# Splitting the second row tile's statistics, issuing the first weights behind a warming product, and a shorter warming, in a one-core spectral filter and gated MLP kernel

## The chip, the cores and the metric

The kernel runs on one core of one Trainium2 chip. The metric is device time in microseconds (us) of one launch. The kernel before takes 171.04 us, the median of three runs from 170.93 to 171.09.

## What is computed

The input is 2048 rows of 512 values in bfloat16. Every row is normalised, and two branches work on the normalised rows: a two-dimensional Fourier filter and a gated feed-forward block with 1792 hidden columns. The result is their sum with the input.

```python
def reference(A_x, A_w_r, A_w_i, B_x, B_w_gate, B_w_up, B_w_down):
    def _A_ref(x, w_r, w_i):
        X = rfft2(x.astype(float32)) * (w_r + 1j * w_i)
        return irfft2(X, s=(S, D)).astype(bfloat16)

    def _B_ref(x, w_gate, w_up, w_down):
        g = einsum("bsd,df->bsf", x, w_gate)
        u = einsum("bsd,df->bsf", x, w_up)
        return einsum("bsf,fd->bsd", gelu(g) * u, w_down)

    x = A_x
    xn = (x - mean(x)) / sqrt(var(x) + 1e-5)
    return x + _A_ref(xn, A_w_r, A_w_i) + _B_ref(xn, B_w_gate, B_w_up, B_w_down)
```

## The kernel before

The 2048 rows are 16 row tiles of 128 rows; four row tiles make a block. A row tile passes through these steps: a load (`rows`, issued at L461), its mean and variance (`stats`: bn_stats at L511, bn_aggr at L512), the reciprocal root of the variance, the normalising (L528), and a transposition, which puts the 512 columns on the partitions as `xnT`. From `xnT` TensorE makes the gate and up products (L722 for the first three hidden chunks of the first two row tiles, L703 for all others), ScalarE takes them out of PSUM (GELU of the gate at L736 and L708, a copy of the up product at L737 and L709), VectorE multiplies them (L738, L710), and the down products follow (L751). The Fourier branch is short matrix products (L612, L835, L839, L916, L917, L976) with ScalarE evictions and long VectorE butterflies (all recorded at the helper line L465).

No order is written out by hand. Each step is one `op` with an engine, a planned cost, a key and what it reads and writes; `_Sched.run` gives every engine a fixed order from these, and `emit` puts in the semaphore waits. For a load, `land` is a planned landing time: it shapes the order and is no wait. A change of a cost, a key or a dependency can so reorder instructions far from its place.

The start is what the change touches:

- `warm` (L474): products of a constant with itself, ten of 512 columns and one of 256, which nobody reads. They run on TensorE before its first input has arrived.
- Queue of ScalarE: the identity for the transpositions, then the first weights, `wg` and `wu` with 384 columns each (`wload`, 384 KB each), then the Sqrt table, with no wait between the three loads.
- Queue of SP: row tiles 0 and 1 at once; row tiles 2 and 3 behind the fourth warming product (`gate`), then the following weight columns 384 to 768, 768 to 1024 and 1024 to 1280.
- Row tile 0: `root_act` takes the root on ScalarE (L516) and the reciprocal on VectorE (L518). `first_half` normalises half of the columns (L561), transposes them on TensorE (L558) and copies them to `xnT`, the first half on VectorE (L566), the second on ScalarE (L564).
- Row tile 1: `stats`, `root_act`, `norm` (L528), `turn` (transposes at L541, copy at L546), and then its products at L722.
- The GELU table is loaded on ScalarE at L626.

The order of VectorE at the start is: bn_stats and bn_aggr of tile 0, bn_stats of tile 1, reciprocal of tile 0, bn_aggr of tile 1, two half normalisings of tile 0, reciprocal of tile 1, copy of tile 0's first half, normalising of tile 1, copy of tile 1. The order of TensorE is: warming, four transposes of tile 0, two gate products, four transposes of tile 1, the other 22 products of tile 0 (gate chunks 0 to 2, then up chunks 0 to 2), 24 products of tile 1, then L703.

Of the kernel before, what the change touches and what calls it, by code (L numbers as in the profile page):

```python
# [10 lines left out]
F32 = mybir.dt.float32  # L11
# [5 lines left out]
NFC = 14  # L17
NHALF = 10
NFIRST = 3
WARM = 10 * (512,) + (256,)  # L20
HKEY = 1.5
NORM = 20.0, 1.5
STAT = 18.0, 1.5
# [121 lines left out]
class _Sched:  # L145
# [11 lines left out]
    def op(self, eng, cost, fn, reads=(), writes=(), tiles=(), key=0.0, after=(), dma=0, lag=0.0, due=None, land=None):  # L157
        o = _Op()
        o.eng, o.fn, o.cost, o.key, o.dma, o.lag, o.due, o.land = eng, fn, cost, key, dma, lag, due, land
        o.reads, o.writes, o.tiles = reads, writes, [(t, False) for t in tiles]  # L160
        o.extra = [a for a in after if a is not None]
        o.seq = len(self.ops)
        o.end = None
        o.pos = None
        self.ops.append(o)
        return o
# [182 lines left out]
def bass_parallel_sum__spectral_gfnet__glu_gated_geglu__prompt_kernel(  # L349
# [21 lines left out]
    sch = _Sched()  # L371
    op = sch.op

    with ExitStack() as es:
        def sb(name, shape, dt=BF16, cell=0):
            n = int(np.prod(shape))
            t = es.enter_context(nc.sbuf_tensor(name, [P, n], dt))
            return view(t, name, 0, shape, cell)

        def view(t, name, lo, shape, cell=0):  # L380
            n = int(np.prod(shape))
            ap = t[:, lo:lo + n]
            if len(shape) > 1:
                names = "abcdef"[:len(shape)]
                ap = ap.rearrange("p (%s) -> p %s" % (" ".join(names), " ".join(names)), **dict(zip(names[1:], shape[1:])))
            return _V(ap, name, np.arange(lo, lo + n).reshape(shape), cell or (64 if n > 512 else 1))
# [7 lines left out]
        wg = sb("wg", [4, FF])  # L394
# [9 lines left out]
        t2 = sb("edge2", [2, 4, 2])  # L404
        eps = sb("eps", [1], F32)
        bst = sb("bst", [16, 6], F32)
        bag = sb("bag", [16, 2], F32)
        vv = sb("vpe", [16], F32)
        rs = sb("rstd", [16], F32)
# [63 lines left out]
        def warm(n):  # L473
            return op("pe", 0.000834 * n, lambda e: e.matmul(ps_dn[:, 0:n], ones[:, 0:P], ones[:, 0:n], start=True, stop=True), tiles=(wt,), key=-50)  # L474

        warms = [warm(n) for n in WARM]


        def load(q, dst, src, nbytes, **kw):
            return dma(q, dst, lambda: src, nbytes, wr=(dst,), **kw)  # L480

        def wload(q, dst, src, lo, hi, **kw):
            return load(q, dst[:, :, lo:hi], src[:, :, lo:hi], (hi - lo) * 1024, **kw)

        k = iter(np.arange(0.0, 1.0, 0.001))
        def rows(lo, hi, land=None):
            return load("sp", x[:, lo:hi], xb[:, lo:hi, :], (hi - lo) * 131072, key=next(k), land=land)

        load("act", ident, c_small.ap()[:, 0:P], 32768, key=-9)
        for w, v in ((wg, wgv), (wu, wuv)):  # L490
            wload("act", w, v, 0, 384, key=0.5, land=5.5 if w is wg else 6.4)
        rows(0, 1, 3.1)
        rows(1, 2, 3.6)
        gate.append(warms[3])
        rows(2, 3, 6.9)
        rows(3, 4, 7.2)
# [7 lines left out]
        def xs(s):  # L504
            return x[:, s]

        def xn(s):
            return RB(8192 + 512 * (s % 8), [4, P])

        def stats(s, key, due=None, after=()):  # L510
            op("dve", 0.61, lambda e: e.bn_stats(bst[:, s].ap, xs(s).ap), reads=(xs(s),), writes=(bst[:, s],), key=key, due=due, after=after)  # L511
            op("dve", 0.11, lambda e: e.bn_aggr(bag[:, s].ap, bst[:, s].ap), reads=(bst[:, s],), writes=(bag[:, s],), key=key, due=due)  # L512

        def root_act(s0, n, key):
            sl = slice(s0, s0 + n)
            op("act", 0.29, lambda e: e.activation(rs.ap[:, sl], bag.ap[:, sl, 1], ACT.Sqrt, bias=eps.ap, scale=1.0),  # L516
               reads=(bag[:, sl], eps), writes=(rs[:, sl],), key=key)
            op("dve", 0.09, lambda e: e.reciprocal(rs.ap[:, sl], rs.ap[:, sl]), reads=(rs[:, sl],), writes=(rs[:, sl],), key=key)  # L518
# [29 lines left out]
        def first_half(h):  # L548
            cs = slice(2 * h, 2 * h + 2)
            i, r, o = xs(0)[:, 256 * h:256 * h + 256], xn(0)[:, cs].rs([256]), xnT[:, 0, 0, cs].rs([256])  # L550
            t = _T("sp")

            def bank():
                return ps_sp_bf[:, t.slot * 2048:t.slot * 2048 + 256]

            def f(e):
                for j in range(2):
                    ins = e.transpose(bank()[:, j * P:(j + 1) * P], xn(0).ap[:, 2 * h + j], ident.ap)  # L558
                return ins

            op("dve", 0.2, lambda e: e.tensor_scalar(r.ap, i.ap, bag.ap[:, 0, 0:1], rs.ap[:, 0:1], SUB, MUL), reads=(i, bag[:, 0], rs[:, 0:1]), writes=(r,), key=-70.0)  # L561
            op("pe", 2 * 0.107, f, reads=(r, ident), tiles=(t,), key=-70.0, lag=0.1)
            if h:
                op("act", 0.27, lambda e: e.activation(o.ap, bank(), ACT.Copy), writes=(o,), tiles=(t,), key=-70.0)  # L564
            else:
                op("dve", 0.2, lambda e: e.tensor_copy(o.ap, bank()), writes=(o,), tiles=(t,), key=-70.0)  # L566

        def turn_dma(s):
            i, o = xn(s), xnT[:, s // 4, s % 4]
            op("sp", 1.25, lambda e: e.dma_start_transpose(o.ap, i.rs([512]).ap), reads=(i,), writes=(o,), dma=425000, key=-5.0, lag=-0.4 if s < 4 else 0.0)  # L570
# [16 lines left out]
        def fold(b):  # L587
# [15 lines left out]
            for p in {0: (), 1: (4, 6), 2: (8, 10), 3: (12, 14, 0, 2)}[b]:  # L603
                t = _T("sp")

                def f_c(e, p=p, t=t):
# [11 lines left out]
                   writes=(yv,), tiles=(t,), key=-0.5)  # L618

        stats(0, -60.0)  # L620
        stats(1, -66.0, None, (sch.ops[-1],))
        root_act(0, 1, -75.0)
        root_act(1, 1, -64.0)
        for h in range(2):
            first_half(h)
        op("act", 1.5, lambda e: e.activation(tmp.ap, eps.ap, ACT.Gelu_apprx_tanh), reads=(eps, xnT[:, 0, 0], rs[:, 0:2]), writes=(tmp,), key=-30.0)  # L626
        norm(1, -60.0)
        turn(1, 1, -60.0)
        for s in (2, 3):
            stats(s, -58.0, None, (sch.ops[-1],))  # L630
# [217 lines left out]
        for ri, f in ((0, ADD), (1, SUB)):  # L848
            op("pool", 0.3, lambda e, ri=ri, f=f: e.tensor_tensor(edge.ap[:, ri], ev[0].ap[:, ri], ev[1].ap[:, ri], f),
               reads=(ev[0][:, ri], ev[1][:, ri]), writes=(edge[:, ri],), key=1.0)  # L850
# [53 lines left out]
        for i, v in enumerate((0, 4, 1, 7, 2, 6, 3, 5)):  # L904
            t = _T("sp")

            def f_i(e, v=v, t=t):
# [15 lines left out]
               writes=(gv,), tiles=(t,), key=-0.5)  # L923
# [104 lines left out]
```

## Time and profile before

One execution was profiled. It took 171.27 us; its span, from the first to the last instruction, is 169.4 us, and the 1.9 us left lie around the span.

| what | profiled execution |
|---|---|
| time | 171.27 us |
| span | 169.4 us |
| TensorE (PE) busy | 165.2 us, 98% |
| VectorE (DVE) busy | 145.7 us, 86% |
| ScalarE (ACT) busy | 107.7 us, 64% |
| GpSimd (POOL) busy | 10.9 us, 6% |
| DMA, mean over the span | 95 GB/s |

PEld is TensorE's loading of weights, which overlaps its products. In a timeline a line has the start in us, the time in us, the engine, the source line, the operation, and what it writes and reads; idle time ahead of it and what ended that stands in square brackets. "SPq" and "ACTq" are the queues in which an engine issues transfers.

### The profile page before, as it was taken

Reading aid. Unit: us, or ns where it says so; the run is one execution under the profiler, and the core shown is the slowest. Engines: PE = TensorE matmul, PEld = TensorE weight load, DVE = VectorE, ACT = ScalarE, POOL = GpSimd, SP = SyncE. Lnnn points to the kernel's source line nnn. Section 1 sums busy time; section 2 is a strip of 40 time slices with the busy share of each in tenths; the row PEclk is TensorE's granted clock in tenths of the full one; section 3 lists DMA queues with packets and bytes.
Section 4 is the critical chain, followed back from the end, with each engine's and each line's share of the span. In section 5 each row is a group of like instructions: output and inputs, shape, how many; then the busy total and the mean of one; then the engine's idle time right before and its main releaser. Section 6 shows DMA issues by size and latency. Waiting matters only on the chain.

```text
span 169.4 us, 2755 instructions
## 1 busy us (share of the span) xinstructions
PE 165.2 (98%) x1019; PEld 88.2 (52%) x1019; DVE 145.7 (86%) x294; ACT 107.7 (64%) x182; POOL 10.9 (6%) x25
## 2 busy tenths in 40 slices
PE   8799999999999999999999999999999999999994
PEld 3488884444554654444444446455444566544443
DVE  2775999998785299999999999999999995999932
ACT  3588886663957966669494639669556399761000
POOL 2040232420000000002000000000000000000000
PEclk9999999999999999999999999999999999999999
DMA  4999999796734436350000000000000000033311
GB/s 142 340 290 198 299 291 100 227 296 128 193 74 95 93 69 134 90 196 12 2 0 0 0 4 0 0 0 4 2 0 0 0 0 4 2 127 119 130 62 62
DMA packets 24927, 16.02 MB, mean 95 GB/s; under 512 B 10957, under 2 KB 24274, under 8 KB 24914
## 3 DMA queue, kind: packets, MB, share of 16 engines
q1 hardware_dynamic: 23714, 15.03, 37.8%
q10 hardware_dynamic: 1200, 0.82, 1.6%
q8 instruction: 8, 0.13, 0.3%
q14 instruction: 5, 0.04, 0.1%
HBM read 11.38 MB, written 2.10 MB: 80 GB/s over the span
## 4 chain that ended last, share of the span: by engine, by line
PE 95%; DMA 2%; DVE 1%; SPq 0%; issue 0%; DVEq 0%
PE ps_gu L703 56%; PE ps_dn L751 21%; PE ps_sp L751 7%; PE ps_sp L612 2%; PE ps_sp L976 2%; DMA x_sb<-in_A_x_dram 2%; PE ps_sp L835 2%; PE ps_gu L722 1%; PE ps_sp L916 1%; PE ps_sp L917 1%; PE ps_dn L722 1%; DVE bst L511 0%; PE ps_sp L839 0%; PE ps_sp L541 0%; SPq L461 0%
## 5 line engine op out<-in xcount | busy, mean ns | idle before, releaser
L703 PE MATMUL ps_gu<-xnT,wu 128*128 128x512 bf16 (+1 forms) x252 | 57.3, 351 | 0.0
L703 PE MATMUL ps_gu<-xnT,wg 128*128 128x512 bf16 (+1 forms) x252 | 57.3, 350 | 0.0
L709 ACT ACTIVATE uu<-ps_gu 128x512 bf16<-128x512 f32 (+1 forms) x63 | 34.5, 548 | 12.5 <-PE ps_gu L703 11.5
L708 ACT ACTIVATE gg<-ps_gu 128x512 bf16<-128x512 f32 (+1 forms) x63 | 34.6, 550 | 11.1 <-PE ps_gu L703 9.6
L751 PE MATMUL ps_dn<-wd,hT 128*128 128x512 bf16 x168 | 39.4, 379 | 0.0
L703 PEld LDWEIGHTS ps_gu<-xnT,wu 128*128 128x128 bf16 x252 | 24.4, 98 | 21.5 <-ACT uu L737 0.2
L703 PEld LDWEIGHTS ps_gu<-xnT,wg 128*128 128x128 bf16 x252 | 24.3, 98 | 21.0 <-issue 0.2
L465 DVE TENSOR_TENSOR specB<-specB 128x512 bf16<-128x512 bf16 (+2 forms) x58 | 33.3, 610 | 0.6 <-ACT specB L981 0.5
L710 DVE TENSOR_TENSOR hT<-gg,uu 128x512 bf16<-128x512 bf16 (+1 forms) x63 | 23.7, 382 | 6.2 <-ACT uu L709 6.1
L751 PEld LDWEIGHTS ps_dn<-wd,hT 128*128 128x128 bf16 x168 | 16.2, 98 | 18.8 <-issue 0.4
L759 ACT ACTIVATE db<-ps_dn 128x512 bf16<-128x512 f32 x12 | 7.2, 597 | 16.1 <-PE ps_dn L751 16.1
L511 DVE BATCH_NORM_STATS2 bst<-x_sb 128x6 f32<-128x512 bf16 x16 | 10.9, 686 | 3.8 <-DMA x_sb<-in_A_x_dram 3.7
L465 DVE TENSOR_TENSOR specC<-specB 128x1024 bf16<-128x1024 bf16 (+2 forms) x18 | 12.4, 714 | 0.3
L751 PE MATMUL ps_sp<-wd,hT 128*128 128x512 bf16 (+2 forms) x70 | 12.3, 337 | 0.0
L465 DVE TENSOR_TENSOR specB<-specA 128x2048 bf16<-128x2048 bf16 x8 | 9.4, 1218 | 2.3 <-ACT specA L617 2.3
L751 PEld LDWEIGHTS ps_sp<-wd,hT 128*128 128x128 bf16 x70 | 6.3, 97 | 6.1 <-DVE x_sb L762 0.2
L465 DVE TENSOR_TENSOR specB<-specB,filt 128x2048 bf16<-128x2048 bf16 x8 | 9.4, 1220 | 0.0
L617 ACT ACTIVATE specA<-ps_sp 128x1024 bf16<-128x1024 f32 x8 | 7.9, 1028 | 1.7 <-PE ps_sp L612 1.7
L844 ACT ACTIVATE specA<-ps_sp 128x1024 bf16<-128x1024 f32 x8 | 7.9, 1039 | 1.3 <-PE ps_sp L835 1.3
L981 ACT ACTIVATE specB<-ps_sp 128x1024 bf16<-128x1024 f32 x8 | 8.0, 1038 | 0.0
L922 ACT ACTIVATE specC<-ps_sp 128x1024 bf16<-128x1024 f32 x8 | 7.8, 1043 | 0.0
L465 DVE TENSOR_TENSOR specA<-specB 128x2048 bf16<-128x2048 bf16 (+1 forms) x8 | 7.6, 986 | 0.1
(68 smaller groups left out, 121.8 us busy)
## 6 DMA issues: line engine op xcount, KB each, us to landing
out_dram<-x_sb SPq DMA_DIRECT2D x15, 128.0 KB, 1.8
wd<-in_B_w_down_dram SPq DMA_DIRECT2D x1, 1792.0 KB, 8.6
x_sb<-in_A_x_dram SPq DMA_DIRECT2D x3, 512.0 KB, 7.8
toki<-c_ti SPq DMA_DIRECT2D x1, 768.0 KB, 4.4
tokf<-c_tf SPq DMA_DIRECT2D x1, 576.0 KB, 4.1
x_sb<-in_A_x_dram SPq DMA_DIRECT2D x4, 128.0 KB, 3.9
wg<-in_B_w_gate_dram SPq DMA_DIRECT2D x2, 256.0 KB, 6.7
wu<-in_B_w_up_dram SPq DMA_DIRECT2D x2, 256.0 KB, 6.3
```

The lines of the kernel that those rows point to most:

```text
L465: return op("dve", c_tt(n), lambda e: e.tensor_tensor(o.ap, a.ap, b.ap, f), reads=(a, b), writes=(o,), key=key, **kw)
L511: op("dve", 0.61, lambda e: e.bn_stats(bst[:, s].ap, xs(s).ap), reads=(xs(s),), writes=(bst[:, s],), key=key, due=due, after=after)
L617: op("act", c_act(1024), lambda e, yv=yv, t=t: e.activation(yv.ap, spair(t).rearrange("p (s r i) -> p s i r", s=4, r=4), ACT.Copy), writes ...
L703: ins = e.matmul(gub(t, n), w.ap[:, dc, fc * P:(fc + 1) * P], xnT.ap[:, b, sl, dc, :], start=(dc == 0), stop=(dc == 3))
L708: op("act", c_act(n), lambda e: e.activation(gg.ap[:, gs.slot, 0:n], gub(g, n), ACT.Gelu_apprx_tanh), tiles=(g, gs), key=0.0)
L709: op("act", c_act(n), lambda e: e.activation(uu.ap[:, us.slot, 0:n], gub(u, n), ACT.Copy), tiles=(u, us), key=0.0)
L710: op("dve", c_tt(n), lambda e: e.tensor_tensor(hT.ap[:, h.slot, lo:lo + n], gg.ap[:, gs.slot, 0:n], uu.ap[:, us.slot, 0:n], MUL), tiles=(g ...
L751: ins = e.matmul(bank(), hT.ap[:, hs[(b, fc)].slot, sl * P:(sl + 1) * P], wd.ap[:, fc, lo:lo + n], start=(fc == 0), stop=(fc == NFC - 1))
L759: op("act", c_act(n), lambda e: e.activation(db.ap[:, d.slot, 0:n], bank(), ACT.Copy), tiles=(t, d), key=0.0)
L844: op("act", c_act(1024), lambda e, xv=xv, t=t: e.activation(xv.ap, spair(t), ACT.Copy), writes=(xv,), tiles=(t,), key=-0.5)
L922: op("act", c_act(1024), lambda e, gv=gv, t=t: e.activation(gv.ap, spair(t).rearrange("p (k x i) -> p k x i", k=4, x=4), ACT.Copy), writes ...
L981: op("act", c_act(1024), lambda e, rv=rv, t=t: e.activation(rv.ap, spair(t), ACT.Copy), writes=(rv,), tiles=(t,), key=-0.5)
```

## The change

Row tile 1's bn_stats is cut into two halves of 256 columns with an own buffer `bst1`. The first stands behind bn_aggr of tile 0, the second behind both half normalisings of tile 0; one bn_aggr takes both, and its key moves it, tile 1's root and the reciprocal behind tile 0's copy. The load of the first gate weights waits for the first warming product (the up weights are queued behind it), the warming ends after ten products, and the planned landing of tile 1 is moved from 3.6 to 4.0.

```diff
-WARM = 10 * (512,) + (256,)
+WARM = 10 * (512,)
...
+        bst1 = sb("bst1", [12], F32)
...
         for w, v in ((wg, wgv), (wu, wuv)):
-            wload("act", w, v, 0, 384, key=0.5, land=5.5 if w is wg else 6.4)
+            wload("act", w, v, 0, 384, key=0.5, land=5.5 if w is wg else 6.4, after=(warms[0],))
         rows(0, 1, 3.1)
-        rows(1, 2, 3.6)
+        rows(1, 2, 4.0)
...
+        def half_stats(h, key, after):
+            o, i = bst1[:, 6 * h:6 * h + 6], xs(1)[:, 256 * h:256 * h + 256]
+            op("dve", 0.34, lambda e: e.bn_stats(o.ap, i.ap), reads=(i,), writes=(o,), key=key, after=after)
...
             op("dve", 0.2, lambda e: e.tensor_scalar(r.ap, i.ap, bag.ap[:, 0, 0:1], rs.ap[:, 0:1], SUB, MUL), reads=(i, bag[:, 0], rs[:, 0:1]), writes=(r,), key=-70.0)
+            scaled = sch.ops[-1]
...
+            return scaled
...
         stats(0, -60.0)
-        stats(1, -66.0, None, (sch.ops[-1],))
+        half_stats(0, -66.0, (sch.ops[-1],))
         root_act(0, 1, -75.0)
+        scaled = [first_half(h) for h in range(2)]
+        half_stats(1, -71.0, (scaled[1],))
+        op("dve", 0.11, lambda e: e.bn_aggr(bag[:, 1].ap, bst1.ap), reads=(bst1,), writes=(bag[:, 1],), key=-64.0)
         root_act(1, 1, -64.0)
-        for h in range(2):
-            first_half(h)
```

The orders that come out of it differ at the start in these places. VectorE: bn_stats and bn_aggr of tile 0, first half statistics of tile 1, reciprocal of tile 0, two half normalisings of tile 0, second half statistics, copy of tile 0, bn_aggr of tile 1, reciprocal of tile 1, normalising of tile 1, copy of tile 1. ScalarE: root of tile 0, copy of tile 0's second half, root of tile 1 (before, both roots came first). TensorE: the four transposes of tile 1 stand behind the gate products and eight of the twelve up products of tile 0 (before, behind two gate products), and the first L703 groups go gate, up, gate, up (before: gate, gate, up, up). Later in the kernel some groups of the gated block, the down products and the Fourier products change places; their number is the same. POOL's order is the same. In SP's order, far behind the start, one transposing transfer of `mirror` (L585) stands one place earlier and the load of `tokf` one place later.

## The prediction

> **What bounds the kernel now.** I read the page first: busy times and the chain that ended last. TensorE is busy for 98% of the span, so what is left to win is its idle time at the start and the few us after its last product.
>
> ```profile
> PE 165.2 (98%) x1019; PEld 88.2 (52%) x1019; DVE 145.7 (86%) x294; ACT 107.7 (64%) x182; POOL 10.9 (6%) x25
> ```
>
> Then the same chain in order of time (start, us, what). It begins with the load of row tile 1, goes through VectorE to tile 0's first transposes, and stays on TensorE from there to the end.
>
> ```profile
> 1.17 3.35 DMA x_sb<-in_A_x_dram
> ...
> 4.62 0.69 DVE bst L511
> 5.32 0.06 DVE rstd L518
> ...
> 9.78 28.90 PE ps_gu L703 x200
> ```
>
> Tile 1 is not needed for tile 0; it stands in the chain because its bn_stats is queued on VectorE ahead of tile 0's reciprocal. From 9.78 us on TensorE never waits (the waits of PE in 10 to 155 us are an empty list), so a change at the start is worth what it moves the first L703 product. The timeline of this stretch gives the durations:
>
> ```profile
> 4.12 0.29 ACT L516 ACTIVATE rstd<-bag,eps 128x1 f32<-128x1 f32 x1 [0.55 <-DVE bag L512]
> ...
> 5.45 0.57 DVE L561 TENSOR_SCALAR specB<-x_sb,bag,rstd 128x256 bf16<-128x256 bf16 x2
> ...
> 6.15 0.29 DVE L566 COPY xnT<-ps_sp 128x256 bf16<-128x256 bf16 x1
> 6.82 0.40 PE L541 MATMUL ps_sp<-smallc,specB 128*128 128x128 bf16 x4
> 7.25 0.42 DVE L546 COPY xnT<-ps_sp 128x512 bf16<-128x512 bf16 x1 [0.49 <-PE ps_sp L541]
> 7.61 0.61 PE L722 MATMUL ps_gu<-xnT,wu 128*128 128x128 bf16 x8
> 8.28 0.39 PE L722 MATMUL ps_gu<-xnT,wg 128*128 128x128 bf16 x4
> ```
>
> The reader is to see the first up product at 7.61 and the first product of tile 1 at 8.28, 1.03 us after its copy began. Last, the transfers (issue to landing), and the share of both queues in 4.5 to 6.0 us (q10 is ScalarE's, q1 is SP's):
>
> ```profile
> wg<-in_B_w_gate_dram ACTq DMA_DIRECT2D x1, 384.0 KB, 4.5
> wu<-in_B_w_up_dram ACTq DMA_DIRECT2D x1, 384.0 KB, 5.1
> ...
> wu<-in_B_w_up_dram SPq DMA_DIRECT2D x1, 384.0 KB, 6.0
> ```
> ```profile
> q1 hardware_dynamic: 138, 0.13, 26.0%
> q10 hardware_dynamic: 515, 0.38, 75.8%
> ```
>
> With issues at 1.11, 1.67 and 3.98 these land at 5.6, 6.77 and 10.0 us. The DMA engines are full from 3.3 us on (shares of 1.06, 1.02 and 0.99 in the windows to 7 us).
>
> **The change, part by part.**
>
> *Weights behind the first warming product.* SP's issue behind the fourth warming product, which began at 2.04 (0.76 plus three steps of 0.427), came at 2.65: 0.61 later. The first began at 0.76, so wg is issued at 1.37 instead of 1.11, and wu 0.26 later too. Queued behind them on ScalarE is the Sqrt table, 2.29 to 3.57, now to 3.83; the root needs it at 4.12, so 0.29 of cover is left. In return tile 1's packets meet fewer weight packets: in 3.2 to 4.5 us its last 39 of 128 had 6.7% of the engines against 95.8% for the weights. Tile 1's landing is bounded by tile 0's, 3.16 (no contention), and by today's 4.53. I take it below 4.05, nearer to tile 0, which was issued 0.45 earlier. Wu's landing is bounded by no delay (6.77, the engines being full) and by 0.26 at a share of 75.8%, 0.35 (7.12). I take 0.26: 7.03.
>
> *First half of the statistics.* No row shows 256 columns; bounds are the full bn_stats (0.69, next instruction after 0.62) and bn_aggr (0.18 and 0.11). I take the middle: 0.43 and 0.36. bn_aggr of tile 0 runs from 3.91 to 4.09; the half begins 0.04 later, at 4.13, and the reciprocal at 4.49 (the root ends at 4.41 and needs 0.07, so 4.48). Before it was 5.24: 0.75 gained. The half normalisings come at 4.70, tile 0's transposes at 5.82 - 0.75 = 5.07.
>
> *Second half and what is behind it.* It waits for both normalisings, 4.70 + 0.57 + 0.04 = 5.31, and tile 0's copy, ready at 6.15 - 0.75 = 5.40, is queued behind it until 5.67: 0.27 given back. The copy ends at 5.96 and the first gate product starts at 6.02 instead of 6.50; wg, at 5.6 + 0.26 = 5.9, just makes it. Behind the copy come bn_aggr 5.88 to 6.06, root 6.09 to 6.39, reciprocal 6.46 to 6.61, normalising 6.67; tile 1 can be transposed at 6.67 + 0.46 = 7.13.
>
> *TensorE's order.* Now 12 gate products (0.67, at 4 in 0.22), 8 up products, and only then tile 1's transposes. The up products could begin at 6.69 but need wu: 7.03 + 0.06 = 7.09. Before, wu had 0.84 us to spare (7.61 against 6.77). The transposes follow at 7.09 + 0.44 = 7.53, the copy at +0.43 = 7.96, its end at 8.38, tile 1's first product at 8.44. Between lie only 0.22 of transposes and 0.22 of up products, so TensorE idles some 0.47: before, 20 products covered that round trip. 8.44 against 8.28 is 0.16 lost.
>
> *First L703 groups.* They start 1.34 later (9.62 - 8.28), at 9.78. Their second group is now an up product, due at 10.22; its weights land at 10.0 to 10.26, and 10.32 is the worst start. The third group waits for the eviction of the second bank, 10.61 + 0.16 = 10.77 and not before, so up to 0.11 of this is hidden. The GELU table (1.28) follows the second root, 6.39 to 7.7, and its first user comes at 8.93 + 0.16.
>
> *Shorter warming.* 256 columns are about 0.11 us of TensorE at the fast step; it idles after them either way (0.96 before the transposes), so nothing. The cover is this idle time, some 0.4 now.
>
> *Later order.* The same products in another order on an engine that never waits: nothing, if operands are in time; DVE is busy 19.73 to 20.00 of 20 us in each stretch from 60 to 140, so a late one would show as PE idle.
>
> **Sum.** -0.75 + 0.27 at the first product, +0.64 for wu and the round trip behind it: +0.16. A profiled run would go from 171.27 to 171.43; on the median of the runs, 171.04, that is 171.20. With wu at 6.77 the same steps give 8.18, -0.10; with 7.12, +0.25. So the likeliest case has 170.94 to 171.29. What a measurement of this kernel can tell from no change is about 0.2%, 0.34 us: the forecast is no change, on the slow side.
>
> **Rivals.**
>
> *Weights later still, slower.* Place: the wait of the up products; it decides from wu at 7.21 on, and each 0.1 after that costs 0.1. SP's queue gets row tiles 2 and 3 and later weights at the same times as before, so it takes from wu. At half the engines, 0.26 becomes 0.52: wu 7.29, tile 1 at 8.70, +0.42, 171.46. The 75.8% row speaks against it; that the late weights meet all of SP's traffic speaks for it. [...] Chance 20%.
>
> *The clock, slower.* Weight loads of the warming come every 0.43 us until 4.13, where two stand within 0.34:
>
> ```profile
> 3.70 0.15 PEld L474 LDWEIGHTS ps_dn<-const-bfloat16-1.0 128*128 128x128 bf16 x1 [0.28 <-issue]
> 4.13 0.34 PEld L474 LDWEIGHTS ps_dn<-const-bfloat16-1.0 128*128 128x128 bf16 x2 [0.28 <-issue]
> ```
>
> So products run at half pace for 3.41 us (0.76 to 4.17), though the granted clock reads 1.00 throughout. The shorter warming ends at about 4.6. [...] Chance 9%.
>
> *The change doesn't do what it says.* Tile 1 still lands at 4.53: first half 4.62, all 0.49 later than above, tile 1 transposed at 7.62, first product 8.53: +0.25, 171.29; later by 0.1, past the limit. For it: the weights are only 0.26 later. Chance 8%, half of it beyond +0.34.
>
> *Faster.* If wu lands by 6.63, the transposes start at 7.13 and tile 1 at 8.04, -0.24; the second L703 group then waits for weights at 10.0 (10.06 instead of 9.82) and leaves -0.11. To pass -0.34 the half statistics must also be near bn_aggr's 0.11 (another 0.25) and both up loads earlier: -0.4 to -0.48, 170.6. For it: stragglers may go with the contention. Chance 17%, 14% beyond -0.34.
>
> **How the numbers follow.** Forecast 46%. Same: 46 + 4 + 3 = 53%. Slower: 20 + 9 + 4 = 33%. Faster: 14%. The range takes in the faster case and late weights up to +0.75, and leaves out most of the clock's: 170.6 to 171.8.
>
> **What would show it.** Right: wg's issue near 1.37; tile 1's first bn_stats straight behind bn_aggr near 4.13; tile 0's transposes near 5.07 and first gate product near 6.0; an idle gap ahead of the up products until wu lands near 7.0; a second of some 0.47 ahead of tile 1's products near 8.4. Wrong: tile 1 landing after 4.29, first up product by 6.8 or after 7.25, warming steps of 0.43 past 4.17, or PE idle time after 10 us.

## The result and the profile after

The changed kernel takes 172.25 us, the median of six runs from 171.89 to 173.25, against 171.03 us for the kernel before (six runs, 170.93 to 171.09). The ratio is 1.0078, with a 95% interval of 1.0052 to 1.0104: 0.8% slower, where no change (171.2 us) was forecast, and above the range given. The profiled execution took 172.50 us (span 170.4), against 171.27 (169.4).

The page first. TensorE does the same work in the same time; the span has grown around it.

```profile
PE 164.5 (97%) x1006; PEld 88.2 (52%) x1018; DVE 146.0 (86%) x295; ACT 107.9 (63%) x182; POOL 10.8 (6%) x25
```

(The change takes one product of the warming away, and 12 of the 1018 that are left have no record here; both lower the sum against the 165.2 of before.) Then the chain that ended last, in order of time (start, us, what):

```profile
0.76 1.02 PE ps_dn L475 x2
1.82 6.04 DMA wu<-in_B_w_up_dram
...
9.26 1.07 PE ps_gu L730 x16
10.77 28.91 PE ps_gu L711 x200
```

Before, it began with row tile 1 and went through VectorE. Now it begins with the first warming products, behind which the weights are issued, and goes on with the load of the first up weights, which takes 6.04 us from its issue. So the weights are what TensorE's start waits for. The line numbers are 8 higher behind the inserted lines: L703 is now L711, L722 is L730. The timeline shows the rest:

```profile
1.38 0.41 ACTq L462 DMA_DIRECT2D wg<-in_B_w_gate_dram  x1
1.82 0.54 ACTq L462 DMA_DIRECT2D wu<-in_B_w_up_dram  x1
...
4.05 0.43 DVE L517 BATCH_NORM_STATS2 bst<-x_sb 128x6 f32<-128x256 bf16 x1
...
4.98 0.54 PE L563 MATMUL ps_sp<-smallc,specB 128*128 128x128 bf16 x4 [0.36 <-DVE specB L566]
...
5.90 0.61 PE L730 MATMUL ps_gu<-xnT,wg 128*128 128x128 bf16 x8 [0.38 <-DVE xnT L572]
...
7.90 0.62 PE L730 MATMUL ps_gu<-xnT,wu 128*128 128x128 bf16 x8 [1.16 <-DMA wu<-in_B_w_up_dram]
...
8.35 0.39 PE L546 MATMUL ps_sp<-smallc,specB 128*128 128x128 bf16 x4
...
8.78 0.42 DVE L551 COPY xnT<-ps_sp 128x512 bf16<-128x512 bf16 x1 [1.86 <-PE ps_sp L546]
...
9.26 0.40 PE L730 MATMUL ps_gu<-xnT,wg 128*128 128x128 bf16 x4 [0.29 <-DVE xnT L551]
...
10.61 0.60 PE L711 MATMUL ps_gu<-xnT,wg 128*128 128x256 bf16 x4
```

Up to 6 us the change does what it says: the first gate product starts at 5.90 instead of 6.50. Then TensorE stands 1.16 us until the up weights land (1.82 + 6.04 = 7.86), and tile 1's transposes are queued behind the up products, so they come at 8.35 and tile 1's first product at 9.26 (8.28 before). The first L711 product starts at 10.61 instead of 9.62: 0.99 later, as much as the span has grown (170.4 - 169.4 = 1.0).

A second thing is later by the same amount: the first long butterfly of VectorE, which reads the transposed row tiles 2 and 3. Before and after:

```profile
15.91 1.03 DVE L465 TENSOR_TENSOR specB<-xnT 128x1024 bf16<-128x1024 bf16 x2
```
```profile
16.91 0.69 DVE L466 TENSOR_TENSOR specB<-xnT 128x1024 bf16<-128x1024 bf16 x1 [0.90 <-DMA xnT<-specB]
```

VectorE comes to tile 2's statistics only behind tile 1's copy, at 9.24 us instead of 7.71, and the transposing transfers of tiles 2 and 3 follow from there.

The load itself is the odd thing. The windows view (length; busy us of PE, PEld, DVE, ACT, POOL; granted clock; DMA share; GB/s), before:

```profile
3.25:4.75 1.50, 1.50 (x6) 0.52 (x4) 0.93 (x3) 0.62 (x2) 0.00 (x0) 1.00 1.01 312
4.75:8.00 3.25, 2.12 (x29) 1.53 (x28) 2.67 (x10) 1.88 (x3) 0.00 (x0) 1.00 1.05 345
```

and after:

```profile
3.25:4.75 1.50, 1.37 (x5) 0.39 (x3) 1.40 (x5) 0.77 (x2) 0.00 (x0) 1.00 0.83 202
4.75:8.00 3.25, 1.48 (x18) 1.01 (x19) 1.74 (x7) 2.17 (x4) 0.00 (x0) 1.00 0.98 328
```

From 3.25 to 4.75 us 202 GB/s move instead of 312, though the weights were issued only 0.27 and 0.15 us later, and later on the engines move no more than before (328 against 345), so nothing is made up. SP's queue did not take the engines: it moved nothing from 3.25 to 4.75 us. The queues in 4.5 to 6.0 us (packets, MB, share; q10 is ScalarE's, q1 SP's) are, after:

```profile
q10 hardware_dynamic: 590, 0.44, 91.4%
q1 hardware_dynamic: 35, 0.03, 6.4%
```

SP's queue had 26.0% of this stretch before and has 6.4% now: row tiles 2 and 3 are held up as well. In the trace each of these loads ends with 16 completions, as many as there are DMA engines: of the up weights, the middle one came at 6.1 us before and at 6.5 after, the last one at 6.81 and at 7.85. The product waits for the last: it starts at 7.90.

### The profile page after: what moved, and what is told of

Its sections match the earlier page's. It is cut to its first block, busy times and chain, and to the rows that moved or that the text cites. A ratio compares the mean times of both kernels' runs of the same rounds, so it can differ in the third digit from the quotient of the medians.

```text
span 170.4 us, 2744 instructions
## 1 busy us (share of the span) xinstructions
PE 164.5 (97%) x1006; PEld 88.2 (52%) x1018; DVE 146.0 (86%) x295; ACT 107.9 (63%) x182; POOL 10.8 (6%) x25
## 4 chain that ended last, share of the span: by engine, by line
PE 94%; DMA 4%; issue 0%; DVE 0%; ACTq 0%
PE ps_gu L711 56%; PE ps_dn L759 21%; PE ps_sp L759 7%; DMA wu<-in_B_w_up_dram 4%; PE ps_sp L619 2%; PE ps_sp L984 2%; PE ps_sp L843 2%; PE ps_sp L924 1%; PE ps_sp L925 1%; PE ps_gu L730 1%; PE ps_dn L475 1%; PE ps_sp L847 0%; PE ps_dn L730 0%; DVE xnT L551 0%; DVE x_sb L770 0%
## 5 line engine op out<-in xcount | busy, mean ns | idle before, releaser
L711 PE MATMUL ps_gu<-xnT,wu 128*128 128x512 bf16 (+1 forms) x252 | 57.4, 350 | 0.0
L711 PE MATMUL ps_gu<-xnT,wg 128*128 128x512 bf16 (+1 forms) x252 | 57.4, 350 | 0.0
L759 PE MATMUL ps_dn<-wd,hT 128*128 128x512 bf16 x157 | 36.7, 379 | 0.6
L711 PEld LDWEIGHTS ps_gu<-xnT,wg 128*128 128x128 bf16 x252 | 24.3, 98 | 21.7 <-ACT uu L745 0.2
L711 PEld LDWEIGHTS ps_gu<-xnT,wu 128*128 128x128 bf16 x252 | 24.3, 98 | 21.3 <-ACT gg L716 0.4
L512 DVE BATCH_NORM_STATS2 bst<-x_sb 128x6 f32<-128x512 bf16 x15 | 10.2, 686 | 3.7 <-DMA x_sb<-in_A_x_dram 3.6
```

The costliest lines, as they stand in the source:

```text
L711: ins = e.matmul(gub(t, n), w.ap[:, dc, fc * P:(fc + 1) * P], xnT.ap[:, b, sl, dc, :], start=(dc == 0), stop=(dc == 3))
L759: ins = e.matmul(bank(), hT.ap[:, hs[(b, fc)].slot, sl * P:(sl + 1) * P], wd.ap[:, fc, lo:lo + n], start=(fc == 0), stop=(fc == NFC - 1))
```

## The experiments

Two theories stood at the outset. **Weights:** the later issue makes the first weights land late, and all loss follows from it. **Order:** the new order (tile 1's transposes behind the up products, and the later order that comes with it) costs the time whatever the weights do. Each kernel was measured beside runs of the kernel before on the same chip: the first four beside 171.11 us (13 runs), the three from "No wait, and the transposes first" on beside 171.05 us (29 runs), the others beside 171.07 us (14 runs), but for the load of 256 bytes, beside 171.25 us (17 runs).

**The change without the weights' wait.** All orders as in the changed kernel.

```diff
-wload("act", w, v, 0, 384, key=0.5, land=5.5 if w is wg else 6.4, after=(warms[0],))
+wload("act", w, v, 0, 384, key=0.5, land=5.5 if w is wg else 6.4)
```

> The changed kernel with the first weights issued at once again; the orders of TensorE and VectorE are those of the changed kernel. Theory (the delayed weights cost the time: the first up products waited until 7.90 us for wu): wu lands near 6.8 us again, the first up product starts at 6.8 to 7.2, tile 1's first product at 8.2 to 8.55 (against 9.26), and the time is 171.0 to 171.3 us. Rival 1 (the split statistics and the new order cost it): about 172.2. Rival 2 (the shorter warming): about 172.2.

Measured: 172.20 us, ratio 1.0070 (1.0042 to 1.0098). The up weights land at 6.5 us, 341 GB/s move in 3.25 to 4.75 us, and the first L711 product starts at 9.71. Yet the time is not won back: in the profile TensorE loses 0.5 us at 16.5 us and 0.6 at 102.6, where it never waited before. Tile 1's transposes still stand behind the up products, so tile 2's statistics begin at 8.34 instead of 7.71, and the first butterfly starts at 16.41 instead of 15.91.

```profile
102.59 0.23 PE L924 MATMUL ps_sp<-toki,specA 128*128 128x128 bf16 x1 [0.46 <-DVE specA L891]
```

So the wait is not needed for the kernel to be slow, and the theory of the weights alone falls for this order of instructions. This kernel is also a test of the forecast's own case "With wu at 6.77", which gave tile 1's first product at 8.18 and a time 0.10 us below that of before. Tile 1's first product came at 8.36 and the first L711 product only 0.09 later than before, but the time is 1.1 us longer (172.20 against 171.11).

**The kernel before with the weights' wait alone.** All orders as before.

```diff
-wload("act", w, v, 0, 384, key=0.5, land=5.5 if w is wg else 6.4)
+wload("act", w, v, 0, 384, key=0.5, land=5.5 if w is wg else 6.4, after=(warms[0],))
```

> The kernel before with only the first weights behind the first warming product. Theory: wu lands late here too (7.3 to 8.0 us); this order needs it at 7.61, and tile 1's copy is done long before, so only what passes 7.55 costs: 0 to 0.4, 171.0 to 171.4 us. Rival (the late landing in the one profile was chance, wu lands near 7.03 as forecast): 171.0. Rival (the split costs the time): 171.0.

Measured: 171.94 us, ratio 1.0039 (1.0026 to 1.0052). The same wait, no other change, and the same low rate:

```profile
3.25:4.75 1.50, 1.50 (x5) 0.59 (x4) 1.43 (x4) 0.77 (x2) 0.00 (x0) 1.00 0.68 135
```

The up weights land at 7.6 us, but the first L703 product starts at 9.69, only 0.07 later than in the profile of before. The loss comes later, in the first butterfly:

```profile
16.74 1.03 DVE L465 TENSOR_TENSOR specB<-xnT 128x1024 bf16<-128x1024 bf16 x2 [0.56 <-DMA xnT<-specB]
```
```profile
16.81 0.60 PE L703 MATMUL ps_gu<-xnT,wg 128*128 128x256 bf16 x4 [0.50 <-ACT uu L709]
```

VectorE waits for the transposing transfers of tiles 2 and 3, its products of the gated block are queued behind that, ScalarE finds no free buffer for 0.71 us, and TensorE no free bank for 0.50. So the wait alone costs 0.4%, and in this order it shows at the first butterfly and not at TensorE's start.

**Tile 1's transposes ahead of the up products, with the weights' wait.** The planned landing of the up weights is put to 7.6, near the measured one.

```diff
-    wload("act", w, v, 0, 384, key=0.5, land=5.5 if w is wg else 6.4, after=(warms[0],))
+    wload("act", w, v, 0, 384, key=0.5, land=5.5 if w is wg else 7.6, after=(warms[0],))
```

> The changed kernel with a planned landing of 7.6 for wu, which moves tile 1's four transposes ahead of the up products and nothing else at the start. Theory (after the wait for wu, tile 1's transposes and copy lie bare behind it): transposes near 7.0 us under the wait, 12 up products from wu's landing, tile 1's first product 0.67 after that, 0.69 sooner than in the changed kernel: about 171.55 us. Rival (the wait for wu is the whole loss, the round trip is hidden anyway): about 172.2.

Measured: 171.89 us, ratio 1.0052 (1.0032 to 1.0073). The copy of tile 1 is now covered by products, as it was before the change:

```profile
7.39 0.62 PE L730 MATMUL ps_gu<-xnT,wu 128*128 128x128 bf16 x8
7.84 0.39 PE L730 MATMUL ps_dn<-xnT,wu 128*128 128x128 bf16 x4
8.07 0.39 PE L730 MATMUL ps_gu<-xnT,wg 128*128 128x128 bf16 x4
...
10.64 0.61 PE L711 MATMUL ps_gu<-xnT,wu 128*128 128x256 bf16 x4 [0.64 <-DMA wu<-in_B_w_up_dram]
```

From the first up product to tile 1's first product it is 0.68 us (7.39 to 8.07) instead of 1.36 (7.90 to 9.26). But of the 1.2 us by which the first L711 product comes earlier (9.41 against 10.61), more than half is lost at once: the second up weights, on SP's queue, land at 10.6 (10.0 before), and TensorE waits 0.64 us for them.

**Row tiles 2 and 3 later.** Their issue, and what SP's queue has behind them, waits for the eighth warming product instead of the fourth, to take SP's packets out of the weights' way.

```diff
-        gate.append(warms[3])
+        gate.append(warms[7])
```

> The changed kernel with row tiles 2 and 3 behind the eighth warming product instead of the fourth, so that SP issues them some 1.7 us later (near 4.3 us) and the other weights behind them. Theory A (SP's transfers, issued right behind the weights, are what slows wu beyond its 0.15 to 0.26 us of later issue): wu lands near 7.0 us, 171.4 us. Theory B (the weights are slow by themselves): wu lands at 7.7 or later, 172.2 us or more, since the weights of the next chunks come later too.

Measured: 172.56 us, ratio 1.0074 (1.0046 to 1.0102); 173 GB/s in 3.25 to 4.75 us, the up weights at 7.2. With nothing of SP's behind the first two row tiles, the rate is as low. Sharing with SP's queue is not the cause of the low rate.

**No wait, and the transposes first.** The first and third edits together.

```diff
-    wload("act", w, v, 0, 384, key=0.5, land=5.5 if w is wg else 6.4, after=(warms[0],))
+    wload("act", w, v, 0, 384, key=0.5, land=5.5 if w is wg else 7.6)
```

> The changed kernel with the first weights issued at once and tile 1's transposes ahead of the up products (orders as in e3_turn_first). Theory 2 (two chains lead out of the start, TensorE's and the one of row tiles 2 and 3: their bn_stats on VectorE, their transposing transfers on SP's queue, and the first fold near 16 us; each has no slack): tile 1's copy near 7.4 us, bn_stats of tile 2 at 7.8 to 8.1 (7.71 before, 8.34 in e1, 9.24 in the changed kernel), first L703 product at 9.2 to 9.5, so both chains are nearly where they were: 171.0 to 171.4 us. Theory 1 alone (only TensorE's start counts): 170.7 to 171.0. Rival (the split itself costs, wherever TensorE starts): 172 as in e1.

Measured: 171.27 us, ratio 1.0012 (0.9989 to 1.0035). Together they take the loss away: the changed kernel's split statistics and shorter warming, with neither the wait nor the late transposes, cannot be told from the kernel before. They bring no gain either, though the first L711 product starts at 9.25: TensorE loses 0.4 us at 15.9.

**The shorter warming alone**, in the kernel before.

```diff
-WARM = 10 * (512,) + (256,)
+WARM = 10 * (512,)
```

> The kernel before with only the shorter warming; no order changes. Theory: nothing, TensorE idles behind the warming anyway: 171.0 to 171.2 us. Rival (the pace of the products doubles later or not in time when the warming ends earlier): 171.5 to 173, with spread.

Measured: 171.17 us, ratio 1.0013 (0.9988 to 1.0038). The median shows no cost. But one of the ten runs took 173.12 us, as the rival has it; the next section comes back to this. The profile shows an early start that is given back:

```profile
7.82 0.39 PE L722 MATMUL ps_gu<-xnT,wg 128*128 128x128 bf16 x4
...
16.42 0.60 PE L703 MATMUL ps_gu<-xnT,wg 128*128 128x256 bf16 x4 [0.37 <-ACT gg L708]
```

Tile 1 starts 0.46 earlier than in the profile of before, the first L703 product 0.35 earlier (9.27), and TensorE then loses 0.5 us at 10.6 and 0.5 at 16.4, by the starts of its products. The early start is not the work of the shorter warming: row tile 1 landed at 4.07 us here and at 4.53 in the profile of before. In the next kernel, whose edit lies behind the start, it landed at 3.70, and tile 1's first product came at 7.87, the first L703 product at 9.21. The same start so varies by 0.4 us from one profile to another.

**Tile 2's statistics later**: one bn_stats more, which nobody reads, ahead of tile 2's in the kernel before.

```diff
+        bst1 = sb("bst1", [6], F32)
...
+        op("dve", 0.0, lambda e: e.bn_stats(bst1.ap, xs(1).ap), reads=(xs(1),), writes=(bst1,), key=-59.0, after=(sch.ops[-1],))
```

> The kernel before with one more bn_stats of 512 columns, whose result nobody reads, between tile 1's copy and tile 2's bn_stats on VectorE; it is planned at no cost, so all orders stay. TensorE's start is untouched. Theory 2: tile 2's bn_stats 0.62 us later (8.33), both transposing transfers and the next row tiles on SP's queue and the first fold 0.5 to 0.6 later, and TensorE waits some 0.3 to 0.6 us near 16 to 17 us or behind: 171.4 to 171.7 us. Theory 1 (only TensorE's start counts, row tiles 2 and 3 have slack): 171.1.

Measured: 171.21 us, ratio 0.9999 (0.9984 to 1.0013). Tile 2's bn_stats starts at 8.03 instead of 7.71, and the first butterfly at 15.66 instead of 15.91. A statistic that is 0.32 us later is so not enough to make the butterfly late. Over all profiles 5.1 to 8.0 us pass from the issue of the first transposing transfer to the butterfly, so the transfers vary more than their issue.

**Is it the wait or the late issue?** In the kernel before, all orders kept: the weights behind the second warming product; a second load of the constants ahead of them and no wait; and a load of 256 bytes ahead of them and no wait.

```diff
-    wload("act", w, v, 0, 384, key=0.5, land=5.5 if w is wg else 6.4)
+    wload("act", w, v, 0, 384, key=0.5, land=5.5 if w is wg else 6.4, after=(warms[1],))
```

> The kernel before with the first weights behind the second warming product instead of no product; nothing else, every engine's order as before. wg should be issued near 1.80 us and wu near 2.25, 0.43 later than with the wait on the first product. Three theories of why gated weights land late. 'Bare delay' (the landing follows the issue, one for one): wu lands at 6.8 + 0.6 = 7.4 at most, and 300 GB/s or more move in 3.25 to 4.75 us. 'Lead' (the later the issue, the lower the rate of the first 1.5 us of the transfer, whatever delays the issue): fewer than 150 GB/s in 3.25 to 4.75 us, wu at 8.0 or later, the median near 172.3. 'The wait' (an issue that carries a wait has the low rate, however long it waits): wu at 7.6 + 0.4 = 8.0, as with 'lead'; these two are told apart by the next kernel.

```diff
-load("act", ident, c_small.ap()[:, 0:P], 32768, key=-9)
+for o in (sb("ident2", [P]), ident): load("act", o, c_small.ap()[:, 0:P], 32768, key=-9)
```

> The kernel before with the 32 KB load of the constants made twice on ScalarE's queue, the first time into a tile that nobody reads; no wait is added, every engine's order is otherwise as before. By the 0.55 us from the one issue to the next, wg is issued near 1.66 us and wu near 2.2, as late as behind the second warming product. 'Bare delay': wu lands by 7.4 and 300 GB/s or more move in 3.25 to 4.75 us; the up products begin near 7.6 as before, median 171.0 to 171.4. 'Lead': under 200 GB/s in that stretch, wu at 8.0 or later, median 172 or more. 'The wait': no wait, so 300 GB/s or more and wu near 7.3, median 171.0 to 171.4, while the kernel behind the second product is at 8.0.

```diff
-load("act", ident, c_small.ap()[:, 0:P], 32768, key=-9)
+load("act", ident, c_small.ap()[:, 0:P], 32768, key=-9); one = sb("one", [P]); load("act", one[0:1], c_small.ap()[0:1, 0:P], 256, key=-8.5)
...
-op("act", 1.5, lambda e: e.activation(tmp.ap, eps.ap, ACT.Gelu_apprx_tanh), reads=(eps, xnT[:, 0, 0], rs[:, 0:2]), writes=(tmp,), key=-30.0)
+op("act", 1.5, lambda e: e.activation(tmp.ap, eps.ap, ACT.Gelu_apprx_tanh), reads=(eps, xnT[:, 0, 0], rs[:, 0:2], one[0:1]), writes=(tmp,), key=-30.0)
```

> The kernel before with one more load on ScalarE's queue between the constants and the first weights, of 256 bytes into a tile that only the dummy operation of the GELU table names; no wait on TensorE is added, every engine's order is otherwise as before. Loads of one row were issued 0.25 to 0.3 us apart on SyncE's queue in the profile of before, so wg should be issued near 1.38 us and wu near 1.9: as with the wait on the first warming product (1.38 and 1.82), where in four profiles of four wu landed at 7.24 to 7.85 and 135 to 202 GB/s moved in 3.25 to 4.75 us, while issues at 1.66 and 1.81 gave 7.1 or less. 'The moment' (an issue near 1.4 us is the bad one, whatever delays it): under 210 GB/s in that stretch, wu at 7.2 or later, median 171.6 to 172.2. 'The wait on the first product' (the semaphore wait is the cause): 280 GB/s or more and wu at 6.8 to 7.0, median 171.0 to 171.4.

Measured: 171.76 us (ratio 1.0042, 1.0030 to 1.0055), 171.84 us (1.0045, 1.0030 to 1.0060) and 171.74 us (1.0024, 1.0008 to 1.0039). The third missed its aim: its small load took 0.54 us to issue, so the gate weights went at 1.69 and not at 1.38. So it does not tell "the moment" from "the wait on the first product". The two kernels with an extra load are slower without any wait, so a late issue costs time with or without one. Of the three theories of the first two kernels none has its numbers: the up weights landed at 7.1 and 6.8, near "bare delay", at 206 and 247 GB/s, between the theories (7.55 and 216 in the third kernel). TensorE first waits for the second weights. With the extra load:

```profile
9.85 1.05 PE L703 MATMUL ps_gu<-xnT,wg 128*128 128x256 bf16 x8 [0.44 <-DMA wg<-in_B_w_gate_dram]
```

That start is 0.23 us later than before, out of 1.0 by which the span is longer (170.4 against 169.4). TensorE waits again at 11.20 and at 16.93, behind a first butterfly that starts at 16.91 instead of 15.91.

**The weights earlier.** The constants' load goes to SP's queue, behind row tiles 0 and 1; the weights are first on ScalarE's queue. Once in the kernel before, once in the kernel with no wait and the transposes first.

```diff
-        load("act", ident, c_small.ap()[:, 0:P], 32768, key=-9)
...
+        load("sp", ident, c_small.ap()[:, 0:P], 32768, key=next(k), land=3.3)
         gate.append(warms[3])
```

> The kernel before with the 32 KB load of the constants on SyncE's queue, behind the loads of row tiles 0 and 1, instead of first on ScalarE's; the first weights are so issued some 0.55 us earlier (wg near 0.56, wu near 1.1), with no wait; every other order as before. By all theories the rate is at least that of before. If the landing follows the issue, wu lands near 6.3, row tiles 2 and 3 some 0.4 earlier than 7.13 and 7.53, and the second weights 0.4 earlier than 8.73 and 9.95, so that the waits at 10 to 11 and at 16 to 17 us end earlier: 170.6 to 171.0 if TensorE's first product of tile 1 stays at 8.3. The rival: weights that are earlier meet tile 1's packets, it lands at 4.8 to 5.0 instead of 4.53, the first products move with it and the time is 171.2 to 171.5.

> The changed kernel without the weights' wait and with tile 1's transposes ahead of the up products (171.27 when it ran before), and with the constants' load on SyncE's queue as in the kernel just above: the first weights some 0.55 us earlier. If what is left of the loss lies in waits for transfers (second weights at 10 to 11 us, transposing transfers behind tile 2's rows at 16 to 17 us), all of them land earlier and it beats both kernels: 170.4 to 170.9. If tile 1's rows, late by the weights' packets, set the start, its first half of the statistics begins at 4.8 or later, tile 1's first product comes at 8.3 or later, and the time is 171.2 to 171.6.

Measured: 173.57 us (ratio 1.0151, 1.0128 to 1.0174) and 173.28 us (1.0141, 1.0119 to 1.0163): the worst of all. The engines are full from 3.25 to 4.75 us (shares of 1.09 and 1.08), and the up weights land at 6.3 and 6.4 us. But ScalarE's queue had 84.2 and 83.1% of the engines from 3.25 to 4.75 us and SP's 25.1%, and the first rows came later: row tile 1 lands at 5.1 and 5.2 instead of 4.53, and the constants, needed by the first transposes, at 6.6. The rate in the first of the two, and the wait for the constants in the second:

```profile
3.25:4.75 1.50, 1.50 (x5) 0.61 (x4) 0.88 (x2) 0.29 (x1) 0.00 (x0) 1.00 1.09 373
```
```profile
6.71 0.38 PE L563 MATMUL ps_sp<-smallc,specB 128*128 128x128 bf16 x4 [1.53 <-DMA smallc<-c_small]
```

The rival of the expectation came, and dearer than it was priced: the late constants had not been seen. In the profiled run of the first kernel TensorE also ran at half pace until 13 us (four products of one chunk in 0.42 us instead of 0.22), which the last section shows.

The runs side by side, ordered by when the gate weights are issued (us; landings are issue plus time to landing; one profile each; the span is that of the profile, the ratio that of all runs):

| kernel | wg issued | GB/s, 3.25 to 4.75 | wu lands | second wu lands | first L703/L711 | first butterfly | span | ratio |
|---|---|---|---|---|---|---|---|---|
| constants on SP | 0.72 | 373 | 6.3 | 9.7 | 13.07 | 19.23 | 172.7 | 1.0151 |
| the same, transposes first | 0.72 | 369 | 6.4 | 9.7 | 10.72 | 16.83 | 170.4 | 1.0141 |
| before | 1.11 | 312 | 6.8 | 10.0 | 9.62 | 15.91 | 169.4 | 1 |
| shorter warming | 1.11 | 335 | 6.7 | 10.5 | 9.27 | 16.35 | 169.8 | 1.0013 |
| later statistics | 1.11 | 337 | 6.7 | 9.8 | 9.21 | 15.66 | 169.4 | 0.9999 |
| no wait | 1.11 | 341 | 6.5 | 9.7 | 9.71 | 16.41 | 170.7 | 1.0070 |
| no wait, transposes first | 1.11 | 330 | 6.6 | 9.8 | 9.25 | 15.85 | 169.3 | 1.0012 |
| after | 1.38 | 202 | 7.85 | 10.7 | 10.61 | 16.91 | 170.4 | 1.0078 |
| wait alone | 1.38 | 135 | 7.6 | 10.8 | 9.69 | 16.74 | 170.2 | 1.0039 |
| transposes first | 1.38 | 158 | 7.3 | 10.6 | 9.41 | 15.41 | 169.7 | 1.0052 |
| rows later | 1.38 | 173 | 7.2 | 11.35 | 10.18 | 17.24 | 170.7 | 1.0074 |
| extra load | 1.60 | 247 | 6.8 | 11.1 | 9.85 | 16.91 | 170.4 | 1.0045 |
| small load | 1.69 | 216 | 7.55 | 11.2 | 10.01 | 16.92 | 170.5 | 1.0024 |
| second product | 1.81 | 206 | 7.1 | 11.1 | 9.90 | 16.91 | 170.4 | 1.0042 |

All seven kernels that issue the weights later than before move fewer bytes in this stretch and have the second up weights at 10.6 or later; all seven are slower. Of the seven that don't, none has fewer than 312 GB/s, and the second weights land by 10.5; three of these are slower too (no wait, and both with the constants on SP's queue).

The late ones are of two kinds. In the last third of the stretch, 4.25 to 4.75 us, the extra load, the small load and the second product are at 336 to 355 GB/s, as fast as the kernels that issue at 1.11 (312 to 353). They begin later: from 3.25 to 3.75 us they move 77 to 89 GB/s, where those move 266 to 322. The four kernels that wait for the first warming product are still at 178 to 252 there: they stay slow.

The column of the first butterfly goes with the span better than that of the first L703 product. In 11 of the 14 profiles the span is the start of the butterfly plus 153.4 to 153.6 us, while first L703 products at 9.21 and 9.62 stand beside the same span of 169.4. The exceptions are the later statistics (153.7), no wait (154.3, with the 0.6 us lost at 102.6) and the transposes first (154.3, with the wait of 0.64 us for the second up weights). No run moved the butterfly alone, so that it sets the time is read from these profiles and not tried.

## Why the prediction was wrong

**The step that failed is the landing of the up weights:** "Wu's landing is bounded by no delay (6.77, the engines being full) and by 0.26 at a share of 75.8%, 0.35 (7.12). I take 0.26: 7.03." The issue of wg was right to 0.01 us (1.38, with 1.37 forecast) and that of wu was 0.11 earlier than forecast (1.82, with 1.93), but wu landed at 7.85, 0.82 later than taken and 0.73 outside its bounds. Both bounds came from a profile in which the load had started in time, and scaled a delay of the issue by a share of the engines. That the rate itself would change was not among the bounds.

**The other steps up to tile 1's first product held.** One by one: tile 1's rows landed at 3.59 (forecast: before 4.05), the half statistics took 0.43 us and began at 4.05 (0.43, 4.13), tile 0's transposes came at 4.98 (5.07), the second half at 5.21 (5.31), the first gate product at 5.90 (6.02). The bare round trip of tile 1's transposes and copy left TensorE idle 0.46 us by the products' starts, with 0.47 forecast, and moving the transposes ahead of the up products took it away. Put the measured landing into the forecast's sum and it gives 0.16 + 0.82 = 0.98, and 0.98 was measured at tile 1's first product (9.26 against 8.28). That it fits so closely is partly luck: 8.28 is the latest of this point in three profiles with the start of before or nearly so (7.82 with the shorter warming, 7.87 with the later statistics), because row tile 1 landed late in it, and the forecast counted its gain of 0.75 from there.

**The rival "Weights later still" had the place and the point from which it decides,** but neither size nor cause. Its 0.52 came from sharing with SP's queue, with half of the engines for the weights. That half was the author's estimate, and no run shows it: in the changed kernel SP's queue moved nothing from 3.25 to 4.75 us and had 6.4% of 4.5 to 6.0 us (26.0% before), and the up weights landed 1.05 us later (7.85 against 6.80). With SP's loads held back the rate stayed low (173 GB/s).

**The rival "The clock" did not come in the profiled run, but a trace of it stands in the times.** In the changed kernel the step of the warming falls below 0.43 us behind 3.70, before the 4.17 of the prediction. That moment is not fixed: in the profile of the later statistics, whose warming is that of before, the eleven products of it take 4.64 us, from 0.76 to 5.40, and 4.10 us in the profile of before. And in that of no wait with the transposes first, eight gate products take 0.82 us, where they take 0.61 in the changed kernel:

```profile
5.89 0.82 PE L730 MATMUL ps_gu<-xnT,wg 128*128 128x128 bf16 x8 [0.26 <-DVE xnT L572]
```

Five of the six kernels with the shorter warming and the constants in their place have one run at 173.03 to 173.25 us, 0.8 to 2.0 us above their medians: 5 of 44 runs with the sixth, whose slowest is at 172.88. Of the 124 runs of the kernels with the full warming and the constants in their place, that of before among them, none is above 172.38. On the chip where the shorter warming ran alone (slowest 173.12), the slowest of 29 runs of the kernel before took 171.91. So the shorter warming goes with 0.8 to 2 us more in about one run of nine, which a median hides. No profile of such a run exists, so that the pace is the reason is not shown. How much a slower pace would cost (the range leaves out "most of the clock's") was the author's estimate, and no run shows that either; the 0.8 to 2 us are what the runs showed.

**A second step failed: "a change at the start is worth what it moves the first L703 product".** In the changed kernel it fits (0.99 and 1.0), but the kernel without the wait shows that this is not all: there the first L711 product moved by 0.09 and the time by 1.1. The path through row tiles 2 and 3, their statistics on VectorE, their transposing transfers and the first butterfly, was put at nothing, without a reason. An empty list of waits behind 10 us meant that these waits were not met at that start, not that they are far away. In the profile of the shorter warming TensorE began 0.35 earlier and lost it at 10.6 and 16.4; in that of the wait alone it began 0.07 later and the kernel lost 0.4%. Behind the first products stand the second weights at 10 to 11 us and the transposing transfers of tiles 2 and 3 at 16 to 17 us, both at the end of the same row of loads. This fits that no faster start among these kernels beat the kernel before, and that the losses don't add: the wait alone costs 0.4%, the rest without the wait 0.7%, both 0.8%.

**"Later order: nothing if operands are in time"** held in the changed kernel (the waits of TensorE from 10 to 155 us are an empty list) but not in the profile of its order without the wait, which lost 0.6 us at 102.6. With the transposes first and no wait, that loss is gone. One profile each doesn't show whether the wait hides a cost of the order or this loss comes and goes.

What stays open is why the weights issued at 1.38 us, behind the first warming product, move so slowly until 4.75 us. It isn't SP's row tiles. A wait as such is not enough: behind the second product the load begins later and then runs at 346 GB/s from 4.25 to 4.75 us, as those do that are late without a wait. But no kernel issued the weights at 1.38 without that wait, so the moment and the wait on the first product are not told apart.

The lost bytes explain part of the delay of the second weights. Up to 4.75 us the profile of before moved 160 GB/s on average, the one with the wait alone 113, which is 47 x 4.75 = 223 KB or 0.65 us at the 342 GB/s of the time after, and its second up weights landed 0.8 later. With the extra load the average is 150, which by the same reckoning gives 0.14 us, and its second up weights landed 1.1 later. There most of the delay is the spread between the 16 completions of the load: the eighth is 0.45 later than before (9.75 against 9.30), the last 1.1 (11.06 against 9.95). What makes the spread was not tried.

## What to carry to other kernels

Where the DMA engines are full from 3.3 us on, as here, what they don't move in the first microseconds can be missing at the last load of the row (with the wait alone 0.65 us by the bytes, of 0.8 measured). So price a delayed issue by the last load of that row and by its last completion, and not by the share of a queue at its middle. Ask of a start which later step on another engine waits for it too: here the first butterfly went with the time better than TensorE's first products (11 of 14 profiles within 0.2 us). Issuing a load later, to let a smaller one pass, and issuing it earlier both lost here: such a start is best changed by one issue at a time, with the rate of the first stretch read from the profile each time. A trace without waits says where the waits are not, but how near the next one is has to be asked of each load and buffer behind the start, since a gain in front of it can be given back there. And one profile of a start is one draw: the same start lay 0.4 us apart in two profiles.

## What the hardware showed beyond that

- Seven late issues in seven moved 135 to 247 GB/s in 3.25 to 4.75 us, five at 1.11 us 312 to 341, two at 0.72 us 369 and 373. It is no smooth function of the issue: 1.38 us was worse (135 to 202) than 1.60 to 1.81 (206 to 247). The stretch is fixed, so for the later issues part of it lies ahead of the load's full rate (77 to 89 GB/s from 3.25 to 3.75 us at the three latest, 336 to 355 from 4.25 to 4.75).
- A full bn_stats of 512 columns takes 0.69 us, one of 256 columns 0.43: as an estimate from these two, 0.17 of it doesn't shrink with the columns (0.43 - 0.26).
- TensorE's products ran at half pace for long in one profile. With the constants on SP's queue, the four products of one chunk took 0.42 us instead of 0.22 until 13 us, at a granted clock that reads 1.00, in the slowest of its runs (174.59 us):

```profile
12.65 0.63 PE L722 MATMUL ps_dn<-xnT,wu 128*128 128x128 bf16 x4
13.07 1.08 PE L703 MATMUL ps_gu<-xnT,wg 128*128 128x256 bf16 x8
```

  The other kernel with the constants on SP's queue had an even longer idle gap ahead of its transposes (1.53 us against 1.29) and ran them in 0.38 us, against 0.59. What decides it was not tried.
